# A spectral mixer beside a gated MLP on one core: the order of moments, folds and roots, and the last output column in two halves

## The chip, the cores and the metric

The kernel runs on one core of a Trainium2 chip. The metric is the device time in microseconds, 186.8 us before the change (median of 3 runs, 186.73 to 187.27). Engines work side by side, each through its own queue in order: TensorE (PE; PEld is its weight load), VectorE (DVE), ScalarE (ACT), GpSimd (POOL), and SyncE (SP), which issues nearly all DMAs. Matmuls write to PSUM and only DVE and ACT take results out of it here.

## The reference

The input x has 2048 rows and 512 features. Its rows are normalised, and two things are computed of the result and added to x: a filter in the frequency domain and a gated MLP.

```python
def _A_ref(x, w_r, w_i):
    X = rfft2(x.astype(float32), axes=(-2, -1))
    X = X * (w_r + 1j * w_i)
    return irfft2(X, s=(S, D), axes=(-2, -1)).astype(bfloat16)

def _B_ref(x, w_gate, w_up, w_down):       # 512 -> 1792 -> 512
    g = jnp.einsum("bsd,df->bsf", x, w_gate)
    u = jnp.einsum("bsd,df->bsf", x, w_up)
    return jnp.einsum("bsf,fd->bsd", _gelu(g) * u, w_down)

x = A_x
xn = _layernorm(x, axis=-1)
return x + _A_ref(xn, A_w_r, A_w_i) + _B_ref(xn, B_w_gate, B_w_up, B_w_down)
```

## The kernel before

The 2048 rows are 16 "columns" of 128 rows (row 16p + c lies in partition p of column c). All of x stays on the core as x_t, its normalised form as xn, and xnT0 to xnT3 hold the transposes, four columns each.

**Normalisation.** `moments(c)` takes mean and variance of a column on DVE (a statistics and an aggregate instruction, lines 257 and 258). `scales` makes the reciprocal roots of the variances of several columns by `rsqrt`: a first guess from the bits and three Newton steps, on POOL 16 instructions with the last two (lines 235 to 248, 264, 265), whatever the number of columns. `normalize(c)` writes xn, for c of 4 and more on ACT (line 273). `transposes` goes through PE for the first four columns, and for the others by a transposing DMA of SP, one per column (line 310). Columns 0 and 1 are done at once, 2 and 3 together, 4 to 15 in three batches of four.

**The MLP.** `glu(c0, n, fc)` makes one unit: 128 of the 1792 hidden features for n columns. Four matmuls into g_ps (line 477), four into u_ps (480), the GELU on ACT (483), and the product into hT on DVE (484). g_ps and u_ps have two buffers each, so unit k+2 waits for the GELU and the product of unit k. Units of one column come first, then of two, then of four. Of the last kind six read xnT0; the next 14 read xnT1, then 14 xnT2, then 14 xnT3. "Unit 7" below is the first that reads xnT1, "unit 21" the first that reads xnT2.

**The filter.** `fold(cg)` makes sums and differences of mirrored features of four columns, in four DVE instructions (A at lines 320 and 321, xf at 323 and 325); A has one buffer. `pstep(cg, q)` is four matmuls into bp (line 333), and ACT casts them to Bs (339). When all 16 psteps are done, eight rounds follow of `dstep` (dp, line 346, cast to ds), `cstep` (ep, line 358, cast to E in four ACT instructions), `filt` (DVE, with the filter's tables TW, ending in the DMA copies of F) and `icstep` (gp, line 430, cast to Gs). bp, dp, ep, gp, yp and y_ps share the PSUM tag "S" with four buffers.

**The end.** `idstep(c)` takes the filter's result of a column out of Gs (yp, line 445). `down(c)` adds 14 matmuls of the down projection (y_ps, 490) and one for the filter's last transform (492), loads x again (494), adds it on DVE (495) and stores the column on SP (496).

**The order.** The units run in a fixed order. A list of tasks, each with a due time counted in the time of GLU units (1.724 for a unit of four columns), is sorted, and before each unit the tasks that are due are written out. A scheduler then sets each engine's order from this and its own model of time, except for the instructions kept in program order (statistics and normalisations among them). The tile pools settle the buffers: `pw` has two of each name unless told otherwise, `pc` one.

Of the kernel before, what the change touches and what calls it, by code (L numbers as in the profile page):

```python
# [10 lines left out]
P = 128  # L11
BF16 = mybir.dt.bfloat16
F32 = mybir.dt.float32
I32 = mybir.dt.int32
ALU = mybir.AluOpType
AF = mybir.ActivationFunctionType

S = 2048
D = 512
NC = 16  # L20
# [3 lines left out]
NFC = DF // P  # L24
# [99 lines left out]
def kernel(  # L124
# [11 lines left out]
    nc = tc.nc  # L136
# [6 lines left out]
    out_v = out.rearrange("b (p c) d -> p c (b d)", c=NC)  # L143
# [4 lines left out]
    pc = ctx.enter_context(tc.tile_pool(name="pc", bufs=1))  # L148
    ps = ctx.enter_context(tc.tile_pool(name="ps", bufs=2, space=bass.MemoryType.PSUM))
    pw = ctx.enter_context(tc.tile_pool(name="pw", bufs=2))  # L150
# [5 lines left out]
    Wd_sb = pc.tile([P, NFC, D], BF16, name="Wd_sb")  # L156
# [4 lines left out]
    late = {}  # L161
# [68 lines left out]

    def rsqrt(V, y, var, n):

        v = pw.tile([P, n], F32, name=f"v{n}")
        t = pw.tile([P, n], F32, name=f"t{n}")
        V.tensor_scalar(out=v[:], in0=var, scalar1=EPS, scalar2=None, op0=ALU.add)
        vi, yi = v[:].bitcast(I32), y.bitcast(I32)
        V.tensor_scalar(out=yi, in0=vi, scalar1=-0.5, scalar2=float(0x5F3759DF), op0=ALU.mult, op1=ALU.add)
        for _ in range(3):
            V.tensor_tensor(out=t[:], in0=y, in1=y, op=ALU.mult)
            if V is nc.vector:  # L240
                V.scalar_tensor_tensor(out=t[:], in0=v[:], scalar=-0.5, in1=t[:],
                                       op0=ALU.mult, op1=ALU.mult)
                V.scalar_tensor_tensor(out=y, in0=t[:], scalar=1.5, in1=y,
                                       op0=ALU.add, op1=ALU.mult)
                continue
            V.tensor_tensor(out=t[:], in0=v[:], in1=t[:], op=ALU.mult)
            V.tensor_scalar(out=t[:], in0=t[:], scalar1=-0.5, scalar2=1.5, op0=ALU.mult, op1=ALU.add)
            V.tensor_tensor(out=y, in0=t[:], in1=y, op=ALU.mult)
# [5 lines left out]
    def moments(c):  # L254
        V = nc.vector
        stats = pw.tile([P, V.BN_STATS_DIM], F32, name="stats")
        tc.keep_in_program_order(V.bn_stats(out=stats[:], in_=x_t[:, c, :]))  # L257
        V.bn_aggr(out=mv[:, c, :], in_=stats[:])

    def scales(V, c0, n):  # L260
        r, b = rstd[:, c0:c0 + n], nb[:, c0:c0 + n]
        rsqrt(V, r, mv[:, c0:c0 + n, 1], n)
        if c0 >= 4:
            V.tensor_tensor(out=b, in0=mv[:, c0:c0 + n, 0], in1=r, op=ALU.mult)
            V.tensor_scalar(out=b, in0=b, scalar1=-1.0, scalar2=None, op0=ALU.mult)  # L265

    def normalize(c):
        if c < 4:
            nc.vector.tensor_scalar(out=xn[:, c, :], in0=x_t[:, c, :], scalar1=mv[:, c, 0:1],
                                    scalar2=rstd[:, c:c + 1], op0=ALU.subtract, op1=ALU.mult)  # L270
        else:
            tc.keep_in_program_order(
                nc.scalar.activation(out=xn[:, c, :], in_=x_t[:, c, :], func=AF.Identity,  # L273
                                     bias=nb[:, c:c + 1], scale=rstd[:, c:c + 1]))
# [26 lines left out]
    def transposes(c0, n):  # L301
        if c0 < 4:
            tp = ps.tile([P, NE, n, P], BF16, name="tp", tag="S", bufs=4)
            for j in range(n):
                for e in range(NE):
                    nc.tensor.transpose(tp[:, e, j, :], xn[:, c0 + j, e * P:(e + 1) * P], ident)  # L306
            return nc.vector.tensor_copy(out=xnT[0][:, :, c0:c0 + n, :], in_=tp[:])  # L307
        else:
            for j in range(c0, c0 + n):
                nc.sync.dma_start_transpose(out=xnT[j // 4][:, :, j % 4, :], in_=xn[:, j, :])  # L310
# [4 lines left out]
    def fold(cg):  # L315
        V = nc.vector
        xs = xn[:, 4 * cg:4 * cg + 4, :]
        lo, hi = xs[:, :, 0:256], xs[:, :, 511:255:-1]
        A = pw.tile([P, 4, 2, 256], BF16, name="A", bufs=1)
        V.tensor_tensor(out=A[:, :, 0, :], in0=lo, in1=hi, op=ALU.add)  # L320
        V.tensor_tensor(out=A[:, :, 1, :], in0=lo, in1=hi, op=ALU.subtract)
        xf = pw.tile([P, 4, 4, P], BF16, name="xf")
        V.tensor_tensor(out=xf[:, :, 0:4:3, :], in0=A[:, :, :, 0:128], in1=A[:, :, :, 255:127:-1],  # L323
                        op=ALU.add)
        V.tensor_tensor(out=xf[:, :, 2:0:-1, :], in0=A[:, :, :, 0:128], in1=A[:, :, :, 255:127:-1],
                        op=ALU.subtract)
        fold_out[cg] = xf

    def pstep(cg, q):
        xf = fold_out[cg]  # L330
        bp = ps.tile([P, 4, P], F32, name="bp", tag="S", bufs=4)
        for j in range(4):
            nc.tensor.matmul(bp[:, j], lhsT=xf[:, j, q, :], rhs=RF_t[:, 4 * cg + j, :],  # L333
                             start=True, stop=True)
        o = Bs[:, q].rearrange("p g c r a -> p (c r) g a")[:, 8 * cg:8 * cg + 8]
        evac(o, bp[:].rearrange("p c (r g a) -> p (c r) g a", r=2, a=4))
# [125 lines left out]
    hT = {}  # L462
# [22 lines left out]

    def down(c):
        sb, cl = c // 4, c % 4
        y_ps = ps.tile([P, D], F32, name="y_ps", tag="S", bufs=4)
        for f in range(NFC):
            nc.tensor.matmul(y_ps[:], lhsT=hT[sb, f][:, cl * P:(cl + 1) * P], rhs=Wd_sb[:, f, :],  # L490
                             start=(f == 0), stop=False)
        nc.tensor.matmul(y_ps[:], lhsT=late["RI"][:, c, :], rhs=late["yt"][:, c, :], start=False, stop=True)  # L492
        y_sb = pw.tile([P, D], BF16, name="y_sb", bufs=3)
        nc.sync.dma_start(out=y_sb[:], in_=x_v[:, c, :])
        nc.vector.tensor_tensor(out=y_sb[:], in0=y_ps[:], in1=y_sb[:], op=ALU.add)  # L495
        nc.sync.dma_start(out=out_v[:, c, :], in_=y_sb[:])


    first_columns()
# [11 lines left out]


    tasks = [(20, load_tables), (28, gather_tables)]
    for c0, tm, ts, tx in ((4, 6, 9.5, 14.3), (8, 15, 18.5, 23.5), (12, 19, 23, 28)):
        for c in range(c0, c0 + 4):
            j = c - c0
            tasks.append((tm + 0.8 * j, lambda c=c: moments(c)))
            tasks.append((tx + 0.9 * j, lambda c=c: (normalize(c), transposes(c, 1))))
        tasks.append((ts, lambda c0=c0: scales(nc.gpsimd, c0, 4)))
    for cg in range(4):  # L520
        t = (12, 22, 29.5, 34)[cg]
        tasks.append((t, lambda cg=cg: fold(cg)))
        for q in range(4):
            tasks.append((t + (3 + q if cg < 2 else 1.5 + 0.6 * q), lambda cg=cg, q=q: pstep(cg, q)))
    tasks.append((36, tables_fix))
    t0, dt = 39.5, 5.5
    for i, g in enumerate((1, 2, 3, 4, 5, 6, 7, 0)):
        tasks.append((t0 + dt * i, lambda g=g: dstep(2 * g)))
        tasks.append((t0 + dt * i + 1, lambda g=g: dstep(2 * g + 1)))
# [15 lines left out]
    for c in range(NC + 2):  # L545
        if c < NC:
            idstep(c)
        if c >= 2:
            down(c - 2)
# [30 lines left out]
```

## Time and profile before

| what | value |
|---|---|
| profiled execution | 186.8 us, its span 185.0 us |
| PE busy | 170.8 us (92%), 1062 matmuls |
| DVE, ACT, POOL busy | 116.3, 97.7, 20.5 us |
| granted TensorE clock | full, in all slices |
| DMA | 19.38 MB, mean 105 GB/s |
| one GELU / product / normalisation, 128x512 | 604 / 684 / 824 ns |
| one statistics / aggregate instruction | 669 / 173 ns |
| one fold instruction, 128x1024 | 678 to 686 ns |
| final sum y_sb, 128x512 | 692 ns |
| store of a column, issue to landing | 1.7 us |

The span is the time from the first to the last event of the core; the device time lies 1.8 us above it. Durations of instructions that follow each other on DVE and ACT overlap by about a tenth of a microsecond in the records, so the starts stand closer than the means. The end of a matmul is modelled, and a few matmul records are missing: starts of groups are the safer measure. In lines of the timeline the bracket at the end gives the idle time of the engine just before, and what released it.

### The profile page before, as it was taken

Reading aid. Unit: us, or ns where it says so; the run is one execution under the profiler, and the core shown is the slowest. Engines: PE = TensorE matmul, PEld = TensorE weight load, DVE = VectorE, ACT = ScalarE, POOL = GpSimd, SP = SyncE. Lnnn points to the kernel's source line nnn. Section 1 sums busy time; section 2 is a strip of 40 time slices with the busy share of each in tenths; the row PEclk is TensorE's granted clock in tenths of the full one; section 3 lists DMA queues with packets and bytes.
Section 4 is the critical chain, followed back from the end, with each engine's and each line's share of the span. In section 5 each row is a group of like instructions: output and inputs, shape, how many; then the busy total and the mean of one; then the engine's idle time right before and its main releaser. Section 6 shows DMA issues by size and latency. Waiting matters only on the chain.

```text
span 185.0 us, 3057 instructions
## 1 busy us (share of the span) xinstructions
PE 170.8 (92%) x1062; PEld 93.0 (50%) x1080; DVE 116.3 (63%) x273; ACT 97.7 (53%) x181; POOL 20.5 (11%) x68
## 2 busy tenths in 40 slices
PE   0699999988699999999999999999999999999992
PEld 0588865443355455555545554555544544544440
DVE  1779966965772298697797799844632632632611
ACT  2533449529987778689889886645211211211100
POOL 0000260377753000000000000000000000000000
PEclk9999999999999999999999999999999999999999
DMA  4999963204993002112069112110113221231210
GB/s 139 323 383 384 341 171 62 57 0 85 244 186 115 0 0 56 31 32 57 14 198 299 35 28 57 32 28 2 55 33 113 85 82 60 60 111 59 85 57 28
DMA packets 22063, 19.38 MB, mean 105 GB/s; under 512 B 8288, under 2 KB 20576, under 8 KB 22048
## 3 DMA queue, kind: packets, MB, share of 16 engines
q1 hardware_dynamic: 20816, 17.22, 32.1%
q0 software_dynamic: 416, 1.32, 2.7%
q10 hardware_dynamic: 816, 0.66, 1.2%
q8 instruction: 8, 0.13, 0.3%
q14 instruction: 7, 0.06, 0.1%
HBM read 13.41 MB, written 2.10 MB: 84 GB/s over the span
## 4 chain that ended last, share of the span: by engine, by line
PE 85%; DVE 4%; issue 3%; POOL 2%; ACT 2%; DMA 2%; ACTq 0%
PE y_ps L490 26%; PE g_ps L477 23%; PE u_ps L480 23%; PE yp L445 2%; PE dp L346 2%; PE gp L430 2%; PE ep L358 2%; PE y_ps L492 2%; DMA x_t<-in_A_x_dram 2%; PE bp L333 2%; PE tp L306 1%; DVE hT L484 1%; ACT ge L483 1%; DVE stats L284 1%; ACT Bs L339 1%
## 5 line engine op out<-in xcount | busy, mean ns | idle before, releaser
L480 PE MATMUL u_ps<-xnT,Wu_sb 128*128 128x512 bf16 (+2 forms) x276 | 60.9, 344 | 1.1 <-DVE hT L484 0.9
L477 PE MATMUL g_ps<-xnT,Wg_sb 128*128 128x512 bf16 (+2 forms) x264 | 60.1, 345 | 1.4 <-DVE xnT L307 0.5
L484 DVE TENSOR_TENSOR hT<-u_ps,ge 128x512 bf16<-128x512 f32 (+2 forms) x69 | 40.1, 583 | 18.6 <-PE u_ps L480 10.5
L490 PE MATMUL y_ps<-Wd_sb,hT 128*128 128x512 bf16 x219 | 50.5, 379 | 0.2
L483 ACT ACTIVATE ge<-g_ps 128x512 bf16<-128x512 f32 (+2 forms) x69 | 35.7, 522 | 19.8 <-PE g_ps L477 18.6
L480 PEld LDWEIGHTS <-Wu_sb 128*128 128x128 bf16 x276 | 26.6, 101 | 24.8 <-issue 1.6
L477 PEld LDWEIGHTS <-Wg_sb 128*128 128x128 bf16 x276 | 25.7, 102 | 17.8 <-issue 0.9
L490 PEld LDWEIGHTS <-hT 128*128 128x128 bf16 x224 | 21.3, 98 | 23.1
L495 DVE TENSOR_TENSOR y_sb<-y_ps,y_sb 128x512 bf16<-128x512 f32 x16 | 11.1, 692 | 30.2 <-PE y_ps L492 29.1
L451 ACT CAST yf<-yp 128x512 bf16<-128x512 f32 x16 | 9.2, 588 | 37.3 <-PE yp L445 37.3
L361 ACT CAST E<-ep 64x512 bf16<-64x512 f32 x32 | 18.6, 580 | 4.2 <-PE ep L358 3.9
L273 ACT ACTIVATE xn<-x_t,nb,rstd 128x512 bf16<-128x512 bf16 x12 | 9.6, 824 | 4.8 <-POOL nb L265 4.8
L339 ACT CAST ds<-dp 128x512 bf16<-128x512 f32 x16 | 9.2, 604 | 1.8 <-PE dp L346 1.8
L339 ACT CAST Bs<-bp 128x512 bf16<-128x512 f32 x16 | 9.1, 593 | 1.0 <-PE bp L333 1.0
L339 ACT CAST Gs<-gp 128x512 bf16<-128x512 f32 x16 | 8.6, 591 | 1.4 <-PE gp L430 1.4
L257 DVE BATCH_NORM_STATS2 stats<-x_t 128x6 f32<-128x512 bf16 x14 | 9.3, 669 | 0.0
L383 DVE TENSOR_TENSOR X<-E 128x512 bf16<-128x512 bf16 x8 | 3.4, 425 | 8.3 <-ACT E L361 8.3
L306 PE MATMUL tp<-CT,xn 128*128 128x128 bf16 x16 | 1.9, 264 | 5.9 <-DVE xn L291 5.8
L333 PE MATMUL bp<-RF_t,xf 128*128 128x128 bf16 x64 | 5.4, 219 | 1.8 <-DVE xf L323 1.8
L333 PEld LDWEIGHTS <-xf 128*128 128x128 bf16 x64 | 4.4, 98 | 4.7 <-DVE xf L323 2.3
L445 PEld LDWEIGHTS <-Gs 128*128 128x128 bf16 x64 | 4.8, 98 | 3.3
L445 PE MATMUL yp<-CT,Gs 128*128 128x128 bf16 x64 | 5.9, 219 | 0.1
(67 smaller groups left out, 124.6 us busy)
## 6 DMA issues: line engine op xcount, KB each, us to landing
y_sb<-in_A_x_dram SPq DMA_DIRECT2D x16, 128.0 KB, 2.1
F<-F SPq DMA_DIRECT2D x32, 64.0 KB, 2.0
out_dram<-y_sb SPq DMA_DIRECT2D x16, 128.0 KB, 1.7
Wd_sb<-in_B_w_down_dram SPq DMA_DIRECT2D x1, 1792.0 KB, 9.2
x_t<-in_A_x_dram SPq DMA_DIRECT2D x3, 512.0 KB, 11.6
Wg_sb<-in_B_w_gate_dram SPq DMA_DIRECT2D x1, 768.0 KB, 9.1
Wu_sb<-in_B_w_up_dram SPq DMA_DIRECT2D x1, 768.0 KB, 10.7
Wg_sb<-in_B_w_gate_dram SPq DMA_DIRECT2D x2, 256.0 KB, 5.3
```

The source lines that it names most:

```text
L257: tc.keep_in_program_order(V.bn_stats(out=stats[:], in_=x_t[:, c, :]))
L273: nc.scalar.activation(out=xn[:, c, :], in_=x_t[:, c, :], func=AF.Identity, bias=nb[:, c:c + 1], scale=rstd[:, c:c + 1]))
L333: nc.tensor.matmul(bp[:, j], lhsT=xf[:, j, q, :], rhs=RF_t[:, 4 * cg + j, :], start=True, stop=True)
L339: nc.scalar.copy(out=o, in_=i)
L361: nc.scalar.copy(out=E[64 * h:64 * h + 64, r], in_=ep[64 * r:64 * r + 64])
L445: nc.tensor.matmul(yp[:, q], lhsT=Gs[:, q, c], rhs=IQ[q], start=(q == 0), stop=(q == 3), skip_group_check=True)
L477: nc.tensor.matmul(gp[:], lhsT=Wg_sb[:, e, fc * P:(fc + 1) * P], rhs=rhs[:, e, :], start=(e == 0), stop=(e == NE - 1))
L480: nc.tensor.matmul(up[:], lhsT=Wu_sb[:, e, fc * P:(fc + 1) * P], rhs=rhs[:, e, :], start=(e == 0), stop=(e == NE - 1))
L483: nc.scalar.activation(out=ge[:], in_=gp[:], func=AF.Gelu_apprx_tanh)
L484: nc.vector.tensor_tensor(out=hT[sb, fc][:, o:o + w], in0=up[:], in1=ge[:], op=ALU.mult)
L490: nc.tensor.matmul(y_ps[:], lhsT=hT[sb, f][:, cl * P:(cl + 1) * P], rhs=Wd_sb[:, f, :], start=(f == 0), stop=False)
L495: nc.vector.tensor_tensor(out=y_sb[:], in0=y_ps[:], in1=y_sb[:], op=ALU.add)
```

## The change

Four edits:

- the scratch tiles of `rsqrt` come from the pool with one buffer;
- in `down`, the last column (c = 15) runs in two halves of 256 features: each has its own PSUM tile, 15 matmuls, sum and store;
- columns 8 to 15 form one batch, so that there are two batches on POOL, of four and of eight columns, where there were three of four; the moments of columns 4 to 7 are due at 8 to 10.4 in place of 6 to 8.4 and the first fold at 8 in place of 12, ahead of them; the second fold is due at 21 in place of 22, the third at 30.5 in place of 29.5; normalisations move with their batch;
- the filter's rounds start at 38 in place of 39.5.

```diff
     def rsqrt(V, y, var, n):
-        v = pw.tile([P, n], F32, name=f"v{n}")
-        t = pw.tile([P, n], F32, name=f"t{n}")
+        v = pc.tile([P, n], F32, name=f"v{n}")
+        t = pc.tile([P, n], F32, name=f"t{n}")
...
     def down(c):
         sb, cl = c // 4, c % 4
-        y_ps = ps.tile([P, D], F32, name="y_ps", tag="S", bufs=4)
-        for f in range(NFC):
-            nc.tensor.matmul(y_ps[:], lhsT=hT[sb, f][:, cl * P:(cl + 1) * P], rhs=Wd_sb[:, f, :],
-                             start=(f == 0), stop=False)
-        nc.tensor.matmul(y_ps[:], lhsT=late["RI"][:, c, :], rhs=late["yt"][:, c, :], start=False, stop=True)
         y_sb = pw.tile([P, D], BF16, name="y_sb", bufs=3)
         nc.sync.dma_start(out=y_sb[:], in_=x_v[:, c, :])
-        nc.vector.tensor_tensor(out=y_sb[:], in0=y_ps[:], in1=y_sb[:], op=ALU.add)
-        nc.sync.dma_start(out=out_v[:, c, :], in_=y_sb[:])
+        w = D if c < NC - 1 else D // 2
+        for o in range(0, D, w):
+            y_ps = ps.tile([P, w], F32, name="y_ps", tag="S", bufs=4)
+            for f in range(NFC):
+                nc.tensor.matmul(y_ps[:], lhsT=hT[sb, f][:, cl * P:(cl + 1) * P], rhs=Wd_sb[:, f, o:o + w],
+                                 start=(f == 0), stop=False)
+            nc.tensor.matmul(y_ps[:], lhsT=late["RI"][:, c, :], rhs=late["yt"][:, c, o:o + w],
+                             start=False, stop=True)
+            nc.vector.tensor_tensor(out=y_sb[:, o:o + w], in0=y_ps[:], in1=y_sb[:, o:o + w], op=ALU.add)
+            nc.sync.dma_start(out=out_v[:, c, o:o + w], in_=y_sb[:, o:o + w])
...
-    for c0, tm, ts, tx in ((4, 6, 9.5, 14.3), (8, 15, 18.5, 23.5), (12, 19, 23, 28)):
-        for c in range(c0, c0 + 4):
+    for c0, n, t in ((4, 4, 8), (8, 8, 14)):
+        for c in range(c0, c0 + n):
             j = c - c0
-            tasks.append((tm + 0.8 * j, lambda c=c: moments(c)))
-            tasks.append((tx + 0.9 * j, lambda c=c: (normalize(c), transposes(c, 1))))
-        tasks.append((ts, lambda c0=c0: scales(nc.gpsimd, c0, 4)))
+            tasks.append((t + 0.8 * j, lambda c=c: moments(c)))
+            tasks.append((t + n + 5 + 0.9 * j, lambda c=c: (normalize(c), transposes(c, 1))))
+        tasks.append((t + n - 0.5, lambda c0=c0, n=n: scales(nc.gpsimd, c0, n)))
     for cg in range(4):
-        t = (12, 22, 29.5, 34)[cg]
+        t = (8, 21, 30.5, 34)[cg]
...
-    t0, dt = 39.5, 5.5
+    t0, dt = 38, 5.5
```

## The prediction

> **What bounds the kernel now.** I read the busy time by stretch first, then the chain of waits between 24 and 50 us, then the timelines of PE, ACT, POOL and SP there and at the end. In the stretches each line has start:end, length, then busy time (count) of PE, PEld, DVE, ACT, POOL, the clock, the DMA share and GB/s.
>
> ```profile
> 17.48:36.44 18.96, 18.47 (x131) 12.07 (x132) 15.72 (x39) 11.58 (x23) 5.34 (x20) 1.00 0.63 176
> 36.44:68.81 32.37, 29.42 (x179) 14.98 (x181) 19.77 (x37) 24.14 (x43) 14.98 (x45) 1.00 0.39 90
> 68.81:126.00 57.19, 56.82 (x344) 29.42 (x350) 45.97 (x109) 46.05 (x84) 0.00 (x0) 1.00 0.25 70
> 126.00:181.40 55.40, 55.05 (x298) 26.80 (x301) 23.23 (x48) 9.18 (x16) 0.00 (x0) 1.00 0.21 67
> ```
>
> TensorE sets the end. A group of four 512-wide matmuls takes 0.864 us from start to start, four bp or dp matmuls 0.22, an ep matmul 0.216. From 68.81 the 28 remaining GLU units (56 groups, 48.4 us) with 48 dp (2.6), 12 ep (2.6) and 64 gp matmuls (3.5) make 57.1 of the 57.19 us; the tail is full in the same way. Between 36.44 (the first group that reads xnT1) and 68.81 (the first that reads xnT2) the work is 14 units (24.2), 48 bp (2.64), 16 dp (0.88) and 4 ep (0.86): 28.6 of 32.37 us. So 3.8 us are missing there, and 0.4 more just ahead of it. They are all that reordering can win. Their causes, in order of time:
>
> ```profile
> 31.93 0.66 DVE A L320
> 35.16 0.24 POOL v L235
> 40.12 0.24 POOL nb L265
> ...
> 40.39 0.81 ACT L273 ACTIVATE xn<-x_t,nb,rstd 128x512 bf16<-128x512 bf16 x1 [4.02 <-POOL nb L265]
> 41.11 0.57 ACT L483 ACTIVATE ge<-g_ps 128x512 bf16<-128x512 f32 x1
> 45.27 0.69 DVE L320 TENSOR_TENSOR A<-xn 128x1024 bf16<-128x1024 bf16 x1 [0.49 <-ACT xn L273]
> 47.83 0.40 PE L333 MATMUL bp<-RF_t,xf 128*128 128x128 bf16 x4 [1.83 <-DVE xf L323]
> ```
>
> ACT stands at column 8's normalisation for 4.02 us, with a GELU queued behind it, until POOL has the roots. The late GELUs stall PE by fractions; then column 11's normalisation is late, with it the third fold (45.27), and PE waits 1.83 us for it.
>
> **What the Trainium skill says.** "SBUF — State Buffer", Who interferes with whom: a VectorE instruction with two SBUF inputs blocks a GpSimd one that reads SBUF, one with at most one, outside the two-port modes, doesn't. The trace agrees: POOL's L239 takes 0.55 us where it meets a fold instruction (two SBUF inputs), 0.20 beside moments and hT products.
>
> ```profile
> 35.57 0.67 DVE L323 TENSOR_TENSOR xf<-A 128x1024 bf16<-128x1024 bf16 x1
> 35.75 0.55 POOL L239 TENSOR_TENSOR t<-rstd 128x4 f32<-128x4 f32 x1
> 37.22 0.20 POOL L239 TENSOR_TENSOR t<-rstd 128x4 f32<-128x4 f32 x1
> ```
>
> "TensorE: Matmul & The Clock Gate", Back-to-back issue gap: the gap is about N/2.4 + 2.5 ns, hence 216 ns at 512 columns and 109 at 256. The trace has 0.864/4 and 0.435/4 us. "DMA: Bandwidth & Descriptors", Latency and other measured facts: a DMA has about 2 us of fixed cost. Here the 128 KB store lands 1.7 us after its issue, and its packets fill only some 0.4 us of that.
>
> **The change, part by part.** I compared the instruction orders of both kernels engine by engine and walked the new ones with durations of this trace. Up to 17.48 us nothing moves.
>
> *First fold ahead of moments 4 to 7.* On VectorE the fold's last three instructions and the four moments change places; both stretches hold seven hT products, so their sum stays. A fold instruction and its hT take 0.93 us together, a moment, its aggregate and its hT 0.99. From 17.48, three of the first and four of the second put the last aggregate at 24.30, where it was at 21.54: 2.76 us later. The POOL chain of 16 instructions takes 0.28 each where nothing blocks it (40.43 to 44.91, 4.48 us); before, the first batch met three fold instructions (21.63 to 27.16, 5.53). Now none is beside it: 24.39 + 4.48 = 28.87. Column 4's normalisation runs on ACT from 28.93, after the GELU of unit 2, its transpose is issued at 29.77. SP's four issues are its own bound:
>
> ```profile
> 28.04 2.18 SPq L310 DMA_TRANSPOSE xnT<-xn  x1
> 30.32 1.20 SPq L310 DMA_TRANSPOSE xnT<-xn  x1
> 32.93 1.22 SPq L310 DMA_TRANSPOSE xnT<-xn  x1
> ```
>
> The fourth comes 4.89 us after the first and lands 2.4 later. So xnT1 is complete at 29.77 + 4.89 + 2.4 = 37.06; before, at 35.3, 1.1 us ahead of its reader. PE would now reach that reader at 15.56 (first u group of 256) + 10 x 0.87 + 3 x 0.22 (three of the first bp groups come earlier) + 0.435 + 2 x 0.864 + 0.22 + 5 x 1.728 = 35.98. **A new wait of 1.1 us**, with all of PE behind it. If the first issue took 1.2 (the median of the twelve) instead of 2.18 it would be 0.1; what makes it slow isn't shown, and I expect it again. Little would be won by 0.1, since the third fold, below, then ends the wait.
>
> *Moments 8 to 15 and their roots in one batch.* After hT of unit 1 (27.33) eight moments and four hT follow on VectorE without a fold between them. 8 x 0.59 + 8 x 0.1 + 4 x 0.60 = 7.9, and 0.2 where an aggregate directly follows its own moment: from 27.93 the last aggregate ends at 36.07 (before: 39.5). POOL's second and last chain is 8 wide; the 128x8 products at L371 take 0.21 against 0.20 at 128x4, so 16 x 0.29 = 4.64, and it meets the second fold's four instructions (36 to 39 us): 4 x 0.35 = 1.4. It starts at 36.16 and ends at 42.2. Before, the second batch ended at 40.35 and the third at 44.91. The order on ACT matters more: column 8's normalisation stands behind the GELUs of units 7 and 8 and three Bs casts. PE runs unit 7 from 37.1, so these end at about 42.0, and ACT no longer waits.
>
> *The walk on.* ACT takes 0.71 per normalisation, 0.48 per GELU, 0.49 per cast. From 42.23: cast, GELU 9, columns 9 and 10, GELU 10, column 11 (ends 46.62). Third fold: L320 46.66, L321, hT, L323 to 49.15, L325 to 49.75. PE, with units 7 to 12 and 16 bp from 37.1, is at 48.56 after one matmul of unit 13: it waits 0.64 for L323 and 0.16 for L325 (before: 1.83 at this fold). Column 15 ends at 52.62 and GELU 13 at 53.61, so unit 15 waits 0.17 and 0.09, the last fold 0.11; the dp and ep of the first filter step are interleaved with units 16 and 17 and wait for casts, 4 x 0.1. From 37.1: 28.6 + 1.57 = 67.27 for the first xnT2 group, against 68.81. **1.54 us gained.** From there both orders hold the same matmuls.
>
> *Scratch of the roots in the single-buffer pool.* No wait in the walk comes from it: two batches, each with names of its own width. Nothing.
>
> *Starts of the filter steps 1.5 earlier.* Counted in the walk. The gather on POOL moves from 45 to 42 us and beside the transposes; its reader comes past 60. Nothing.
>
> *Last column in halves.* 30 matmuls of 0.109 in place of 15 of 0.216: +0.03. The first half's sum and store run beside the second half's matmuls (1.64 us; the sum is about 0.41, and SP's issue 0.33). After the last matmul:
>
> ```profile
> 181.41 0.69 DVE L495 TENSOR_TENSOR y_sb<-y_ps,y_sb 128x512 bf16<-128x512 f32 x1 [2.54 <-PE y_ps L492]
> 182.13 0.33 SPq L496 DMA_DIRECT2D out_dram<-y_sb  x1
> ```
>
> The sum at 256 columns is not in the trace; the nearest row is hT at 128x256 from PSUM, 413 ns against 684 at 512: -0.28. The last matmul ends 0.11 sooner after its start (272 against 379 ns). The half store saves between nothing (fixed cost) and 0.2 (half of its packets' 0.4); the 64 KB copies F land in 2.0, so a loss of 0.3 can't be excluded. I take -0.1. Sum -0.45, bounds -0.65 and 0.
>
> **Sum.** The profiled execution took 186.8 us with a span of 185.0; the median of the runs is also 186.8. 186.8 - 1.54 - 0.45 = **184.8**.
>
> **Rivals.** (1) *The front gives nothing, only the tail counts.* The wait of 1.1 us at xnT1 grows to 2.6, for instance since the normalisations of columns 5 to 7 come between GELUs that are late themselves. Against it: SP, not ACT, sets the pace (the fourth issue at 34.66, its column ready at 33.4). 186.35. (2) *More is gained.* POOL meets fewer fold instructions, or ACT runs its queue faster: the waits of 1.57 shrink to some 0.7. For it: each of them is a difference of two times a few tenths apart. Against: a GELU can't run before its group. 184.0. (3) *Slower: ACT becomes the bound.* In the walk ACT has no idle time from 42.2 to 53.6, and until the dp stage (58) it runs 8 normalisations, 12 casts and 8 GELUs, with PE's fold, GELU and dp waits all behind it. I let each start before the one ahead has ended. If the new mixture of waits makes them run end to end, they cost 0.10 to 0.12 more each, 28 x 0.11 = 3.1 by the dp stage: 187.9. From 0.07 each (1.99/28) on, the gain is gone. For it: ACT is 24 of 32 us busy there already, and the eight columns now come as one block. Against: in the same mixture before, starts stand 0.72, 0.47, 0.71 and 0.46 apart (40.39 to 42.75), which is what I used. (4) *The halves are not independent*, the second sum waiting for the first store to land: 1.7 us after 180.2 in old times plus issue, about 0.5 late, which takes the tail's gain: 185.3. The order shows no such wait on VectorE's last instruction.
>
> **How the numbers follow.** What I walked, the fourth rival with it (184.3 to 185.8): 0.63. More gained (183.4 to 184.3): 0.12. Front without gain (185.8 to 187.2): 0.12. Slower: 0.13. Low 183.8 cuts half of the second, high 186.8 leaves out the slower case and a little of the third. A measurement here tells 0.3% (0.56 us) from no change, so the gain must pass 186.2: faster 0.76, same 0.11, slower 0.13.
>
> **What would show it.** Right: POOL's first chain without a 0.55; a PE wait of about 1 us for the transposes near 36; no ACT wait of 4 us before column 8; PE waits under 0.7 at the third fold; the first xnT2 group near 67.3; a last sum of 0.41. Wrong: xnT1 landing past 38, column 8 normalised after 43, a PE wait in the filter stretch, or a last store landing later than 1.7 us after issue.

## The result, and the profile after

The changed kernel took 185.39 us (median of four executions, 185.09 to 185.59) against 186.79 before. The ratio is 0.992, 95% interval 0.990 to 0.994. The profiled execution took 185.48 us with a span of 183.7, so it lies 1.32 us below the one before. Measured twice more, at other times and on a chip of its own each time (12 and 6; the first chip isn't known), the same kernel gave 0.992 (0.988 to 0.995) and 1.001 (1.000 to 1.002). What goes with that difference is the main finding of the experiments.

The busy time by stretch of the kernel after, from the same events as before: the first 256-wide u group, the first group that reads xnT1, the first that reads xnT2, the first yp, the last matmul. The columns are start:end, length, then busy time (count) of PE, PEld, DVE, ACT and POOL, the clock, the DMA share and GB/s.

```profile
15.89:37.02 21.13, 20.32 (x150) 13.75 (x149) 18.71 (x47) 12.32 (x24) 3.83 (x17) 1.00 0.65 187
37.02:67.38 30.36, 29.43 (x178) 14.55 (x181) 18.91 (x34) 24.99 (x44) 13.53 (x32) 1.00 0.50 96
67.38:124.57 57.19, 56.82 (x343) 29.28 (x348) 45.46 (x107) 45.13 (x83) 0.00 (x0) 1.00 0.25 70
```

The third stretch has its old length, 57.19 us. The second was 32.21 and is 30.36: 1.85 us shorter. (The prediction began it and ended it at 36.44 and 68.81. The second time came from the chain of waits; the timeline has that group at 68.65, so 0.16 of the forecast gain never existed.) The first stretch was 20.88 us (15.56 to 36.44) and is 21.13, so 0.25 is given back ahead of xnT1. The front gains 1.60.

The three longest PE waits left around the second stretch, the first of them just ahead of it, are these. Timeline of PE, kernel after (last column: idle time before, and what ended it):

```profile
37.02 1.02 PE L477 MATMUL g_ps<-xnT,Wg_sb 128*128 128x512 bf16 x4 [0.76 <-DMA xnT<-xn]
...
49.27 0.40 PE L333 MATMUL bp<-RF_t,xf 128*128 128x128 bf16 x4 [0.62 <-DVE xf L323]
...
54.68 0.81 PE L480 MATMUL u_ps<-xnT,Wu_sb 128*128 128x512 bf16 x3 [0.16 <-DVE hT L484]
```

The predicted waits were 1.1, 0.64 and 0.17. POOL and ACT, kernel after: the first chain of roots runs unblocked (24.76 to 29.25), the second is blocked at its start by the second fold, and ACT stands 0.39 us at column 8 where it stood 4.02.

```profile
25.36 0.20 POOL L239 TENSOR_TENSOR t<-rstd 128x4 f32<-128x4 f32 x1
...
29.02 0.23 POOL L265 TENSOR_SCALAR nb<-nb 128x4 f32<-128x4 f32 x1
36.45 0.60 POOL L235 TENSOR_SCALAR v<-mv 128x8 f32<-128x8 f32 x1 [7.20 <-DVE mv L258]
...
42.05 0.24 POOL L265 TENSOR_SCALAR nb<-nb 128x8 f32<-128x8 f32 x1
...
42.32 0.81 ACT L273 ACTIVATE xn<-x_t,nb,rstd 128x512 bf16<-128x512 bf16 x1 [0.39 <-POOL nb L265]
...
46.72 0.69 DVE L320 TENSOR_TENSOR A<-xn 128x1024 bf16<-128x1024 bf16 x1
```

The last line is the third fold, which now starts at 46.72; before, 45.27. Keep that line in mind: the fold is later than before and PE waits less for it, because its first matmuls were also put later in PE's order, behind six units of the second stretch and one matmul, where they stood behind four units.

At the end, the last sum is halved and the last store starts sooner. Timeline of VectorE, kernel after, the two last sums:

```profile
178.54 0.42 DVE L498 TENSOR_TENSOR y_sb<-y_ps,y_sb 128x256 bf16<-128x256 f32 x1 [0.95 <-PE y_ps L496]
...
180.18 0.42 DVE L498 TENSOR_TENSOR y_sb<-y_ps,y_sb 128x256 bf16<-128x256 f32 x1 [1.21 <-PE y_ps L496]
```

From the start of the last matmul to the end of the span it was 4.00 us (180.99 to 185.00) and is 3.84 (179.87 to 183.71); the first yp to the last matmul is 0.14 longer (55.30 against 55.16). So the tail gives 0.03, where 0.45 was forecast. The whole: -1.60 in front, -0.03 in the tail, and +0.33 because the first 256-wide group started later (15.89 against 15.56). That is -1.30; the span is 1.29 shorter, the device time 1.32.

The later start is not the work of the new order. Up to 11.6 us PE's timelines agree within 0.06 us. The 128-wide matmuls stand 0.107 us apart until 11.9 us before and until 12.6 us after, and 0.056 from there on: TensorE reached its full rate later in that execution. So "full, in all slices" in the table of the profile before doesn't hold for the first 12 us. Over all profiled executions the start of the first 256-wide group varied from 15.2 to 17.3, whatever the kernel.

### The profile page after: what moved, and what is told of

Same layout as the page of the kernel before. It is cut to its first block, busy times and chain, and to the rows that moved or that the text cites. A ratio compares the mean times of both kernels' runs of the same rounds, so it can differ in the third digit from the quotient of the medians.

```text
span 183.7 us, 3076 instructions
## 1 busy us (share of the span) xinstructions
PE 171.3 (93%) x1078; PEld 94.2 (51%) x1095; DVE 116.3 (63%) x274; ACT 97.9 (53%) x181; POOL 17.5 (10%) x52
## 3 DMA queue, kind: packets, MB, share of 16 engines
q0 software_dynamic: 416, 1.32, 3.1%
## 4 chain that ended last, share of the span: by engine, by line
PE 78%; DVE 7%; ACT 5%; issue 4%; POOL 3%; DMA 2%; ACTq 0%
PE y_ps L494 26%; PE u_ps L480 21%; PE g_ps L477 19%; DVE hT L484 2%; PE y_ps L496 2%; PE yp L445 2%; PE dp L346 2%; PE ep L358 2%; PE gp L430 2%; DMA x_t<-in_A_x_dram 2%; ACT xn L273 2%; PE bp L333 1%; ACT Bs L339 1%; ACT E L361 1%; PE tp L306 1%
## 5 line engine op out<-in xcount | busy, mean ns | idle before, releaser
L477 PE MATMUL g_ps<-xnT,Wg_sb 128*128 128x512 bf16 (+2 forms) x266 | 61.3, 346 | 1.6 <-DMA xnT<-xn 0.8
L494 PE MATMUL y_ps<-Wd_sb,hT 128*128 128x512 bf16 (+1 forms) x233 | 50.7, 366 | 0.2
L494 PEld LDWEIGHTS <-hT 128*128 128x128 bf16 x238 | 22.7, 98 | 22.0
L498 DVE TENSOR_TENSOR y_sb<-y_ps,y_sb 128x512 bf16<-128x512 f32 (+1 forms) x17 | 11.2, 660 | 29.8 <-PE y_ps L496 29.8
L257 DVE BATCH_NORM_STATS2 stats<-x_t 128x6 f32<-128x512 bf16 x14 | 9.2, 666 | 0.0
L496 PE MATMUL y_ps<-yt,RI_t 128*128 128x512 bf16 (+1 forms) x17 | 6.2, 366 | 0.1
L346 PE MATMUL dp<-CT,Bs 128*128 128x128 bf16 x64 | 6.0, 219 | 0.1
## 6 DMA issues: line engine op xcount, KB each, us to landing
x_t<-in_A_x_dram SPq DMA_DIRECT2D x3, 512.0 KB, 11.9
```

Source lines behind the costliest of these rows:

```text
L346: nc.tensor.matmul(dp[:, q // 2, q % 2, :], lhsT=Bs[:, q, G].rearrange("p c r a -> p (c r a)"), rhs=FQ[q], start=(q == 0), stop=(q == 3), ...
L477: nc.tensor.matmul(gp[:], lhsT=Wg_sb[:, e, fc * P:(fc + 1) * P], rhs=rhs[:, e, :], start=(e == 0), stop=(e == NE - 1))
L498: nc.vector.tensor_tensor(out=y_sb[:, o:o + w], in0=y_ps[:], in1=y_sb[:, o:o + w], op=ALU.add)
```

## The experiments

Twelve kernels in three groups of four, each group on a chip of its own (9, 6 and 12) beside the kernel before (medians 187.17, 186.93 and 186.96 us): halves_only to fold_only, then after_again, fold_halves, gather_early and pairs, then the rest. Stretch lengths are read off the timelines of one execution each; "end" is the start of the last matmul to the end of the span.

| kernel | ratio to before, 95% interval | first u group to xnT1 | xnT1 to xnT2 | end |
|---|---|---|---|---|
| before | 1 | 20.88 | 32.21 | 4.00 |
| after, first time | 0.992 (0.990 to 0.994) | 21.13 | 30.36 | 3.84 |
| halves_only | 0.996 (0.995 to 0.997) | 20.88 | 32.21 | 3.45 |
| front_only | 1.005 (1.003 to 1.007) | 21.14 | 32.32 | 4.36 |
| merge_only | 1.010 (1.007 to 1.012) | 21.01 | 33.26 | 4.38 |
| fold_only | 0.989 (0.987 to 0.991) | 21.14 | 29.52 | 4.00 |
| after_again | 1.001 (1.000 to 1.002) | 21.12 | 32.05 | 3.83 |
| fold_halves | 0.986 (0.984 to 0.988) | 21.12 | 29.53 | 3.45 |
| gather_early | 1.018 (1.015 to 1.022) | 24.29 | 31.47 | 4.36 |
| pairs | 0.992 (0.991 to 0.994) | 20.75 | 31.39 | 3.44 |
| after_c | 0.992 (0.988 to 0.995) | 21.12 | 30.38 | 3.84 |
| after_plain | 0.991 (0.988 to 0.994) | 21.08 | 30.40 | 3.29 |
| fold_tight | 0.990 (0.987 to 0.993) | 21.13 | 30.69 | 3.45 |
| small_edits | 0.999 (0.998 to 1.000) | 20.85 | 32.21 | 4.00 |

### Tail and front apart

halves_only is the kernel before with the new `down`; front_only is the kernel after with the old one.

> The kernel before with the last column in halves and nothing else. Theory A (the end of the program is longer by some 0.4 us whenever TensorE's program has the 16 additional matmuls, since the last barrier then waits for its queue): the last sum takes 0.42 us in place of 0.69, the last packet follows its issue 1.17 us later in place of 1.32, and the last packet stands 1.9 us ahead of the span's end in place of 1.55; the time is 186.5 to 186.9 us, within 0.3 of the kernel before. Theory B (the longer end was chance of one profiled execution): the span ends 1.5 to 1.6 us after the last packet, and the time is about 186.35 us.

> The changed kernel without the halves. Theory A: the halves give less than 0.2 us in all, so the time is 185.3 to 185.6 us. Theory B: the halves give 0.4 us, so it is about 185.8 us. Both: the first group that reads xnT2 starts as in the changed kernel, 67.4 us by the timeline (give or take 0.3 for a start of the weights that varies).

Measured: halves_only 186.41 us, 0.76 below before (0.5 to 1.0 by the interval). Its trace accounts for 0.42 of that: the end is 0.56 shorter and the matmuls 0.14 longer. The rest is not explained by the trace. The time fits theory B, and the end of 3.45 us refutes A: the additional matmuls (15; the expectation says 16) do not lengthen the end. A longer end stands in the kernels with one batch of eight columns, halves or not (front_only 4.36 and merge_only 4.38 against 4.00 before; after 3.84 where halves alone give 3.45).

The trace shows the place. Among the program's last events, POOL's next-to-last one starts 0.09 us behind the start of the drain ahead of it in before, halves_only, fold_only, fold_halves, pairs, fold_tight and small_edits, and 0.46 or 0.47 in after (all three times), front_only, merge_only and gather_early. In the latter group POOL's program is 16 instructions shorter than before; in pairs it is 16 longer. In after_plain, which has two gathers less besides, it is 0.09 again. So these 0.38 us came and went with the number of POOL's instructions. Why, and what POOL waits for there, the trace doesn't tell. (The short end of after_plain is no gain: its device time lies 2.3 us above its span, in all other kernels 1.8.)

front_only came out 0.9 us slower than before, which no theory had. Its front is the kernel after's, instruction by instruction, yet the second stretch took 32.32 us instead of 30.36. Timelines of ACT and PE, front_only:

```profile
49.32 0.40 PE L333 MATMUL bp<-RF_t,xf 128*128 128x128 bf16 x4 [0.61 <-DVE xf L323]
...
48.52 0.59 ACT L483 ACTIVATE ge<-g_ps 128x512 bf16<-128x512 f32 x1
51.72 0.59 ACT L339 CAST Bs<-bp 128x512 bf16<-128x512 f32 x1 [2.61 <-PE g_ps L477]
52.20 0.81 ACT L273 ACTIVATE xn<-x_t,nb,rstd 128x512 bf16<-128x512 bf16 x1
...
55.72 0.81 PE L477 MATMUL g_ps<-xnT,Wg_sb 128*128 128x512 bf16 x3 [1.89 <-ACT ge L483]
```

The cast at 51.72 reads the bp whose matmuls ran at 49.32, were done by 49.72 by the trace, and were followed on PE by others without a break. In the kernel after the same cast starts 0.44 us after the same matmuls (49.27, 49.71). Here it starts 2.4 us after them. Behind it on ACT stand column 14's normalisation, two casts, column 15's, one more cast and then the GELU that PE needs at 55.72: 1.89 us of PE.

The trace's records of the semaphore that TensorE raises tell more. In the kernel after its updates come at 49.69, 50.33, 50.55, 50.78 and 51.21, each 0.01 to 0.02 us behind the shown end of its group. In front_only the same five come within a quarter of a microsecond, at 51.70, 51.77, 51.83, 51.89 and 51.93, and the next one is on time (52.12). By the trace TensorE did not run late; its signal did. The Trainium skill, "Perfetto Trace Analysis", Tensor Engine Instruction (MATMUL, LD_WEIGHTS), says that the end shown for a matmul is computed from its size, and that the update is pushed when PSUM has acknowledged the writes, which the profile doesn't show. The trace agrees as far as it goes: the shown ends look undisturbed while the update is 2 us late. Whether acknowledgement or signal is late, it can't say.

### Parts of the front apart

merge_only takes the kernel before and gives columns 8 to 15 one batch (with the third fold at 30.5, as after); fold_only takes it and puts the first fold ahead of the moments of columns 4 to 7:

```
merge_only
-    for c0, tm, ts, tx in ((4, 6, 9.5, 14.3), (8, 15, 18.5, 23.5), (12, 19, 23, 28)):
+    for c0, n, tm, ts, tx in ((4, 4, 6, 9.5, 14.3), (8, 8, 14, 21.5, 27)):
...
-        tasks.append((ts, lambda c0=c0: scales(nc.gpsimd, c0, 4)))
+        tasks.append((ts, lambda c0=c0, n=n: scales(nc.gpsimd, c0, n)))
...
-        t = (12, 22, 29.5, 34)[cg]
+        t = (12, 22, 30.5, 34)[cg]
fold_only
-    for c0, tm, ts, tx in ((4, 6, 9.5, 14.3), (8, 15, 18.5, 23.5), (12, 19, 23, 28)):
+    for c0, tm, ts, tx in ((4, 8, 11.5, 17), (8, 15, 18.5, 23.5), (12, 19, 23, 28)):
...
-        t = (12, 22, 29.5, 34)[cg]
+        t = (8, 22, 29.5, 34)[cg]
```

> The kernel before with columns 8 to 15 as one batch of moments and one chain of roots 8 wide; the first batch, the first fold, the scratch, the filter steps' starts and the tail stay as before. Theory C (the gain comes from column 8's normalisation standing behind the GELUs whose groups have ended, and the early fold costs a wait at xnT1): no wait of PE for the transposes near 36 us, ACT's wait at column 8 under 1 us, the first xnT2 group 1.3 to 2 us earlier than before, so 184.8 to 185.5 us. Rival D (POOL's chain freed from the folds is what counts, so the early first fold is needed): the gain is under 0.5 us, 186.3 to 186.8 us.

> The kernel before with the first fold ahead of the moments of columns 4 to 7 (fold at 8, first batch as in the changed kernel); the later columns stay in two batches of four. Theory C: POOL's first chain runs in 4.5 us without a blocked operation, PE waits 0.7 to 1.1 us for the transposes at xnT1, ACT still stands 3 to 4 us at column 8, and the time is that of before or longer, 186.8 to 187.8 us. Rival D: it is faster by 0.5 us or more, under 186.3 us.

Both came out against theory C. merge_only is slower than before, 189.12 us; fold_only is the fastest of its group, 184.67, 2.5 us below before by the medians (2.1 by the ratio). Rival D's number holds, and the early fold is what counts. Stretches and waits of fold_only, from the windows and the timelines of PE, ACT and VectorE:

```profile
36.56:66.08 29.52, 28.58 (x178) 14.86 (x182) 18.90 (x35) 23.62 (x43) 14.50 (x36) 1.00 0.53 99
...
36.56 1.02 PE L477 MATMUL g_ps<-xnT,Wg_sb 128*128 128x512 bf16 x4 [0.77 <-DMA xnT<-xn]
...
45.57 0.40 PE L333 MATMUL bp<-RF_t,xf 128*128 128x128 bf16 x4 [0.84 <-DVE xf L323]
...
38.13 0.81 ACT L273 ACTIVATE xn<-x_t,nb,rstd 128x512 bf16<-128x512 bf16 x1 [2.35 <-POOL nb L265]
...
43.02 0.69 DVE L320 TENSOR_TENSOR A<-xn 128x1024 bf16<-128x1024 bf16 x1 [1.68 <-ACT xn L273]
```

The wait at xnT1 is there (0.77), as with the whole change. ACT still stands at column 8, for 2.35 us, and it costs PE nothing. What moved is the third fold: VectorE starts it at 43.02, before 45.27, after 46.72. The reason is not the one that rival D gives, a chain of roots freed from the folds: the chain of columns 8 to 11 takes 5.25 us here (32.85 to 38.10) and 5.19 before (35.16 to 40.35). It starts earlier, because column 11 has its moments earlier. VectorE, first the kernel before, then fold_only:

```profile
31.93 0.66 DVE L320 TENSOR_TENSOR A<-xn 128x1024 bf16<-128x1024 bf16 x1
33.71 0.68 DVE L257 BATCH_NORM_STATS2 stats<-x_t 128x6 f32<-128x512 bf16 x1
...
31.89 0.66 DVE L257 BATCH_NORM_STATS2 stats<-x_t 128x6 f32<-128x512 bf16 x1
33.88 0.68 DVE L320 TENSOR_TENSOR A<-xn 128x1024 bf16<-128x1024 bf16 x1
```

L257 is column 11's statistics, L320 the second fold. Before, the scheduler put the start of the second fold ahead of column 11; with the first fold moved, it stands behind it, though its own due time is the same. So the edit worked through an order that it doesn't name.

One chain for eight columns starts only when all eight have moments, and ended at 42.29 in the kernel after. There the second stretch is 0.84 us longer than in fold_only (30.36 against 29.52), and the end 0.36 longer (front_only against fold_only, both without halves). These 0.84 belong to all that the change does besides the early fold: the batch of eight, the new due times of the second and third folds, and the filter's start. They were not taken apart on top of fold_only. Nor does the loss stand at the third fold, where PE waits less than in fold_only (0.62 against 0.84), but in short waits at the last fold and the first filter step, 54.7 to 59.8 us, each under 0.2.

merge_only by itself:

```profile
49.23 1.02 PE L477 MATMUL g_ps<-xnT,Wg_sb 128*128 128x512 bf16 x4 [0.49 <-ACT ge L483]
...
52.51 0.40 PE L333 MATMUL bp<-RF_t,xf 128*128 128x128 bf16 x4 [0.80 <-DVE xf L323]
...
58.34 1.24 PE L477 MATMUL g_ps<-xnT,Wg_sb 128*128 128x512 bf16 x5 [1.58 <-ACT ge L483]
```

The last line is the late signal again, at the same place in the program: the cast behind the third fold's first bp starts at 54.35, 1.84 us after its matmuls. Without that wait the stretch would be 31.68 (an estimate: 33.26 less 1.58), half a microsecond below before. So the merge may be worth something, but the early fold shortens the stretch by five times as much (2.69).

The batch of eight also opens the door to the late signal. In before and fold_only columns 8 to 15 are all normalised ahead of the third fold's first cast (in fold_only the last two from 46.21, the cast at 47.62). In after, front_only and merge_only columns 14 and 15 stand behind that cast, and behind them the GELU that PE needs. In fold_only one signal was late too: a cast of the last fold, at 53.26, waits 0.85 us for matmuls that ended at 51.95, and PE loses nothing.

### The change again, and its parts together

fold_halves adds the halves to fold_only.

> The changed kernel once more, on the same chip as the three below. Theory E (in the changed kernel without halves TensorE's semaphore comes 2 us late at the third fold, and this belongs to the order of work there, which the halves don't touch; whether it strikes is a matter of a few hundredths of a us): some executions show it, so the times fall into two groups, near 185.4 and near 187.3 us. Rival F (it depends on the rest of the program, the number of TensorE's instructions among it, and so belongs to one build): all executions lie within 0.5 us of 185.5 us.

> The first fold ahead of the moments of columns 4 to 7, two batches of four for the later columns, and the last column in halves. The two add up if they don't meet: 0.4 to 0.75 us less than with the fold alone, so a ratio to the kernel before of 0.985 to 0.987, 184.0 to 184.4 us. If the late semaphore of TensorE strikes here too, 186 us.

after_again took 187.12 us, no gain at all. Its 22 executions lie between 186.5 and 188.2, so neither theory's pattern: not two groups, and not the first result. Its profile has the late signal:

```profile
50.29 0.40 PE L333 MATMUL bp<-RF_t,xf 128*128 128x128 bf16 x4 [0.61 <-DVE xf L323]
...
56.43 0.81 PE L477 MATMUL g_ps<-xnT,Wg_sb 128*128 128x512 bf16 x3 [1.63 <-ACT ge L483]
```

By the times it strikes in every execution here, and the first time it struck in none. fold_halves on the same chip took 184.20 us, as expected, 1.4% below before. It beats both kernels, and its only PE waits in this part are 0.53 us for xnT1 and 0.64 for the third fold: none for a late signal.

### What the late signal goes with

(An update that is missing in the trace looks like a late one, so only bursts, and updates that an engine visibly waits for, are firm.) In every profile where updates of TensorE's semaphore come late in this part of the program, it is at the time of POOL's gathers of the filter's rows (L212), whose transfers run beside the transposing ones. gather_early is front_only with the gathers between POOL's two chains:

```
-    tasks = [(20, load_tables), (28, gather_tables)]
+    tasks = [(12, load_tables), (12.8, gather_tables)]
```

(the instructions that read the gathered rows are kept in their old place by hand).

> The changed kernel without halves, with POOL's six gathers of the filter's rows between its two chains of roots (29 to 37 us) in place of after them. Theory G (the late semaphore at the third fold comes from the gather's transfers, which meet the transposing ones there: packets of 1.7 us stand at 48.8 us): the wait of 1.9 us for a GELU near 55.7 us is gone, the roots end up to 0.5 us later, and the time is 185.8 to 186.4 us. Rival (the transposes alone do it, or the place in the program): the wait stays, 187.8 to 188.3 us.

The wait near 55.7 us is gone, as theory G has it, and the late updates moved with the gathers: four groups of matmuls ended between 34.93 and 37.52, and the updates that belong to them come at 36.50, 39.56 and 39.62. The transposes of the later columns, alone now, have no late update beside them. But the transposes into xnT1 now run beside the gathers. Timelines of SP and PE, gather_early:

```profile
31.16 6.06 SPq L310 DMA_TRANSPOSE xnT<-xn  x4
...
41.22 1.87 PE L477 MATMUL g_ps<-xnT,Wg_sb 128*128 128x512 bf16 x4 [3.70 <-DMA xnT<-xn]
42.88 1.85 PE L480 MATMUL u_ps<-xnT,Wu_sb 128*128 128x512 bf16 x4
```

SP has issued the four at 37.22 and their reader starts 4.0 us later; in the kernel after the last issue ends at 35.60 and the reader starts 1.4 later. And behind this wait TensorE is slow: the two groups shown start 1.66 us apart, where such groups start 0.864 apart otherwise, and from 41.12 to 44.53 us the granted clock is 0.5. That costs 0.8 us on each of them. So 190.50 us: what was expected of the waits held, the forecast of the time missed the collision that it created.

after_plain takes the kernel after and loads the two large gathers' bytes on SP, early, with plain transfers; it leaves out the reversal of the rows that these gathers make:

```
+            tc.keep_in_program_order(nc.sync.dma_start(out=Tf[:, 8 * W:16 * W], in_=w_in.rearrange("(n r) k -> n (r k)", r=8)[0:P]))
...
-            Tf = T.rearrange("p j k -> p (j k)")
-            gather(Tf[:, 8 * W:16 * W], w_in.rearrange("(n r) k -> n (r k)", r=8), 2)
+            pass
...
-                nc.sync.dma_start_transpose(out=xnT[j // 4][:, :, j % 4, :], in_=xn[:, j, :])
+                tc.keep_in_program_order(nc.sync.dma_start_transpose(out=xnT[j // 4][:, :, j % 4, :], in_=xn[:, j, :]))
```

> The changed kernel a third time, beside the three below. Its ratio to the kernel before was 0.992 the first time and 1.001 the second. Where a semaphore of TensorE is late by over 1 us at the third fold in the profiled execution, the ratio is near 1.00; where none is, near 0.992.

> The changed kernel with its two large gathers (1.05 of 1.32 MB) replaced by plain loads of the same size, issued on SP ahead of the transposes; the four small gathers stay. It leaves out the reversal of the rows of the filter's mirrored half, which only the gathers do, so its output is not the reference's. Theory G (gather beside transposes delays TensorE's semaphores): no semaphore later than 0.5 us between 42 and 55 us, third fold's wait 0.6 us, no wait for a GELU after it, stage from xnT1 to xnT2 30.2 to 30.5 us, and 1.3 to 1.9 us less than the changed kernel if that has the late semaphore in this call. Rival (the transposes alone do it): as the changed kernel, within 0.4 us. Against both: the loads, issued near 17 us, may hold up the last weights and start everything later.

after_c behaved as the first time: ratio 0.992, no late update, and ACT's cast right behind its matmuls:

```profile
49.45 0.58 ACT L339 CAST Bs<-bp 128x512 bf16<-128x512 f32 x1 [0.64 <-PE bp L333]
```

That settles what stands between 0.992 and 1.001: with the late signal the second stretch is 32.05, without it 30.36 and 30.38. after_plain has no late update and 30.40, but on a chip where the kernel after had none either, so it doesn't tell gather from transposes. Two things stay open. One is what holds the signal up: the gathers' transfers, POOL's work of issuing them, or either of these only beside transposes. gather_early, on the chip where the kernel after was hit, is the one piece of evidence that it goes with the gathers. The other is why it strikes at some times only: the groups on chips 9 and 6 show it, the group on chip 12 and the first measurement don't, and chip and time of measurement can't be told apart here.

### Small edits, and two attempts at more

small_edits is the kernel before with the scratch in the single-buffer pool and t0 at 38. pairs is fold_halves with the roots of columns 4 and 5 ahead of the fold, and 6 and 7 behind it. fold_tight is fold_halves with columns 4 to 7 normalised 0.45 apart.

```
pairs
-    for c0, tm, ts, tx in ((4, 8, 11.5, 17), (8, 15, 18.5, 23.5), (12, 19, 23, 28)):
+    for c0, n, tm, ts, tx in ((4, 2, 6, 7.7, 12.5), (6, 2, 9.6, 11.5, 17),
+                              (8, 4, 15, 18.5, 23.5), (12, 4, 19, 23, 28)):
fold_tight
-            tasks.append((tx + 0.9 * j, lambda c=c: (normalize(c), transposes(c, 1))))
+            tasks.append((tx + (0.45 if c0 == 4 else 0.9) * j, lambda c=c: (normalize(c), transposes(c, 1))))
```

> The kernel before with the scratch of the roots in the single-buffer pool and the filter steps starting 1.5 units earlier, nothing else. Prediction's step: nothing, within 0.2 us of the kernel before (ratio 0.999 to 1.001). Rival: the earlier start puts casts of the first filter step between the last fold's casts and GELUs, and costs 0.3 us or more.

> As fold_halves, with the roots of columns 4 to 7 in two pairs, the first pair's moments ahead of the fold. If the wait at xnT1 (0.77 us) is the latest thing in the first stage and column 4's transpose is issued 4 us earlier, the wait goes and 0.5 to 0.8 us are gained over fold_halves: 183.4 to 183.8 us. If the first fold, two moments later, now ends the later chain, it is the same or slower.

> As fold_halves, with columns 4 to 7 normalised 0.45 instead of 0.9 units apart, so that columns 5 and 6 come ahead of a GELU and SP's second transpose need not wait for column 5. If SP's issue rate is what sets xnT1, its wait of 0.53 us shrinks to under 0.2, and the time is 0.2 to 0.5 us below fold_halves (ratio 0.983 to 0.985). But the order behind it changes too: the second fold comes earlier on VectorE, the moments of columns 8 to 15 later; if that delays their roots, column 11 and the third fold are late by as much, and nothing is gained or some is lost (0.986 to 0.992).

small_edits: 186.78 us, ratio 0.999 (0.998 to 1.000), second stretch 32.21 as before. The two edits are worth nothing by themselves.

pairs lost: 185.62 us. The wait at xnT1 is gone (20.75), but column 8 is normalised at 39.51 instead of about 38, and the third fold's wait is back at 1.83, the very figure of the kernel before:

```profile
39.51 0.81 ACT L273 ACTIVATE xn<-x_t,nb,rstd 128x512 bf16<-128x512 bf16 x1 [3.19 <-POOL nb L265]
...
46.95 0.40 PE L333 MATMUL bp<-RF_t,xf 128*128 128x128 bf16 x4 [1.83 <-DVE xf L323]
```

fold_tight, on another chip than fold_halves, lost less by the ratio, 185.18 us, and didn't do what it was meant to. Column 5 still stands behind a GELU (30.71), the wait at xnT1 is 0.75, and the second fold, which moved ahead among the moments, makes column 8 late (39.40) and the third fold's wait 1.18. Its second theory held. In both, what is won at xnT1 is lost at the third fold.

## Why the prediction was right, and where it was not

The direction and the place were right: nearly all the gain is between 15 and 68 us, the third stretch keeps its length, and the time lies in the range. There is luck in that. The measurement happened to be one without the late signal; with it the same kernel took 187.12 us, outside the range. And that so many times of the walk agree to 0.1 us owes something to the start that came 0.33 later: counted from the first u group, those from 42 us on came 0.2 to 0.3 earlier than forecast. Step by step:

- **First fold ahead of the moments.** POOL's chain forecast at 4.48 us took 4.49; the last aggregate moved by 2.80 us against 2.76 (8.61 after the first u group, 5.81 before). The wait at xnT1 was forecast at 1.1 (the sum for PE's arrival comes to 35.94, not 35.98, which changes nothing) and was 0.76. The term that was off is the first transpose's issue, taken as 2.18 us again: it took 1.30, and the second then waited for column 5 on ACT instead.
- **Moments 8 to 15 in one batch.** Every time of the walk is within 0.4 us: chain end 42.29 (42.2), third fold's wait 0.62 (0.64), unit 15's 0.16 (0.17), xnT2's group 67.38 (67.27). But the reason given, "The order on ACT matters more: column 8's normalisation stands behind the GELUs", is wrong as a cause. The walk was of the whole change and couldn't tell its parts apart. fold_only showed that much of ACT's wait at column 8 may stay, and that the early fold alone makes the stretch 2.69 us shorter, by way of column 11's moments; the rest of the change, the batch of eight in it, then costs 0.84 of that.
- **"The gather on POOL moves from 45 to 42 us and beside the transposes; its reader comes past 60. Nothing."** This step failed. The reader was never late, but the gathers' transfers lie over the third fold's first matmuls, and there, in one of three measurements of this kernel, TensorE's signal came up to 2 us late, which takes back the whole gain (ratio 1.001). That the gathers make it late is likely, not shown. In the kernel before, columns 14 and 15 don't stand behind the third fold's first cast on ACT: halves_only, which has that order, on a chip where front_only was hit, seems to have updates late at the same time too, and has the same four PE waits as before.
- **Scratch and filter starts.** Nothing on the kernel before (small_edits). With the batch of eight the earlier filter start was not tested apart.
- **Halves.** The sum was forecast at 0.41 us and took 0.42; the last store landed 1.58 us after its issue instead of 1.70, so -0.12 against -0.1. But the sum of the terms counts one gain twice: the last matmul starts 0.14 later and ends 0.11 sooner after its start, and the +0.03 for the 30 matmuls holds both already. The forecast should have been -0.35. halves_only has -0.56 at the end and +0.14 for the matmuls, so -0.42. In the kernel after, POOL's 0.38 us at the very end hid nearly all of it.
- **The sum.** Forecast -1.54 and -0.45. The front gave -1.60 (of a forecast that mixed two clocks by 0.16), the tail -0.42, POOL's end +0.38, and a later start in this execution +0.33. POOL's end is a term that the forecast doesn't have.
- **Spacing of the matmuls.** N/2.4 + 2.5 ns is what the section of the Trainium skill quoted in the prediction gives for a matmul by itself; for a stream it gives less, about 131 ns at 512 columns. The measurement decides: 0.864/4 = 0.216 us, in streams.
- **Rivals.** The slower case named ACT running its queue end to end. ACT's starts stand 0.72, 0.46 and 0.49 apart as taken, so that mechanism didn't show. The neutral result on one chip came from a wait that no rival had. The larger gain, 184.0, is about what fold_halves reached, by leaving part of the change out.

## What to carry to other kernels

A long wait on an engine with slack, here ACT's 4 us at column 8, is not the thing to remove until the view of the engine that sets the end says so: follow the chain back from PE's own wait (third fold, column 11, roots of columns 8 to 11, their moments), and look at what stands ahead in that chain: here a piece of the second fold, in front of column 11's statistics. Batching a chain of small instructions saves instructions but makes the first consumer wait for the last producer; here the kernel with 16 instructions more on POOL and the roots for four columns some 4 us earlier (fold_only) was the faster one. And an order of work that was measured once, on one chip, should be measured again on others, and tried one part at a time.

## What the runs showed that was not expected

- TensorE's semaphore updates reached the other engines up to 2 us after the matmul's shown end, in a burst about 0.06 us apart, while indirect and transposing transfers ran together (front_only, merge_only and after_again; normally 0.01 to 0.02 us). In that stretch single 4 KB packets of the gathers took up to 1.7 us, in fold_only 2.9, against 0.16 in the median; 1.6 us occurred in the kernel after too, which had no late signal, so long packets alone don't make it.
- The reader of four transposing transfers started 4.0 us after their last issue beside gathers (gather_early), and 1.4 us without them (the kernel after).
- After 3.70 us without matmuls in gather_early the granted TensorE clock was 0.5 for 3.4 us.
- The end of a program was 0.38 us longer or shorter with the number of POOL's instructions: 0.47 us ahead of POOL's next-to-last event with 16 instructions less than before, 0.09 with 18 less, with as many, and with 16 more.
